# Attention followed by two feed-forward layers: clamp, value parts and value means of the attention rewritten

## The chip, the cores and the metric

One core of a Trainium2 chip runs the whole program. The time is device microseconds of one execution; three runs of the kernel before gave 818.24, 821.07 and 824.56 us, median 821.07. The engines are PE (TensorE matmul; PEld is its weight load), DVE (VectorE), ACT (ScalarE), POOL (GpSimd) and SP, which issues all DMAs. SBUF is the working memory, PSUM holds what matmuls write (here eight banks of 512 columns, the tile `bank`).

## The reference

Sixteen heads (2 batches of 8) of 768 tokens and 64 columns. Each query and key is assigned to the nearest of 16 centroids of its head, and a query only sees keys of its own cluster:

```
mask   = q_assign[:, :, :, None] == k_assign[:, :, None, :]
scores = scale * np.matmul(q, k.transpose(0, 1, 3, 2))
scores = np.where(mask, scores, -1000000000.0)
scores = scores - np.max(scores, axis=-1, keepdims=True)
attn   = np.exp(scores)
attn   = attn / (np.sum(attn, axis=-1, keepdims=True) + 1e-09)
x      = np.matmul(attn, v)
```

A query whose cluster holds no key sees all its scores equal, so its output is the mean of v. The result, 1536 tokens by 512, then goes through two layers `g(x @ w_in) @ w_out` with 2048 hidden columns, the first with a PReLU, the second with a rational function.

## The kernel before, in words

**Staging.** The program is a list of operations that a planner written into the kernel (`Sched`) puts in order when the program is built. Each operation names the engines that may run it, a cost on each, and the buffers that it takes. The planner places the operation whose planned start, weighted with a due time (`SC.t`), comes first, and among several engines it takes the one with the earliest planned end plus a bias. `BIAS` adds a fixed amount to DVE wherever DVE is one of several choices. What comes out is one fixed order per engine, and each engine works through its own in order. So a change of one cost, buffer or bias can move rows on every engine.

**Attention, one head `i` after the other.** `operands1`/`operands2` bring queries, keys, one-hot clusters into SBUF tiles by DMA. `max_chunk` (nine per head) multiplies 512 columns into a bank and reduces their maxima on DVE (L665) into the small tile `mp`. `m_chain` reduces `mp` to one maximum per query (L674, `mx`), clamps it (L677, `nm`), marks rows without keys on POOL (L679, `nh`), transposes `nm` on PE (L682) and sends the negated row by DMA into the operand. `st_chunk` (nine per head) computes scores on PE (L705, L706) and their exponential on ACT (L710) into `p32`. `p_split` writes each 128x768 block as a float16 part and a float16 remainder: the cast (L414 on ACT, L416 on POOL) and the subtraction (L722), which may go to DVE or POOL; in this kernel all 96 went to POOL. `pv_tile` (six per head, 18 matmuls each, L790 to L792) multiplies both parts with the value parts, and `pv_fin` divides: L807, L809 and L810 make the reciprocal denominator `rc` from the sum of the row, L812 scales the result from PSUM, L814 overwrites rows without keys with the mean.

**Values, one pair of heads.** `v_split` squares v on ACT (L733), sums v per column on DVE (L737), sums over partitions on PE (L740), makes a power-of-two scale `am` (L745, L748, L751 on DVE, L752 and L755 on POOL), casts the scaled v to float16 (L765 on ACT or L767 on POOL) and takes the remainder on DVE (L770). `x_T` transposes the finished pair into x.

**Feed-forward.** 96 steps: `emit_h` (L1033, 12 matmuls of 512 columns) and `emit_y` (L1102, 12 matmuls), with the weights prepared by `w_prep` on ACT, DVE and POOL (L996, L1002, L1004, L1006, L1009, L1016). The first weights are prepared while the last heads of the attention still run, and a few `emit_h` matmuls stand in PE's order ahead of the last transposes of `x_T` (L830).

## Time and profile before

| | |
|---|---|
| median of three runs | 821.07 us (818.24 to 824.56) |
| profiled execution | 825.44 us, its span 823.4 us |
| granted PE clock, mean | 0.965 of full speed |
| busy share of the span | PE 93%, DVE 74%, ACT 69%, POOL 72% |
| chain that ended last, by line | L1102 31%, L1033 30% |

The profile is of one execution of its own. PE's ends are modelled, so a busy PE is not a PE at its peak; how fast it works is read from the distance between the starts of its matmuls. The heads can be followed on DVE by the sixteen L674 (one per head, 35.9 to 253.7 us) and L807 (68.3 to 301.4 us).

### The profile page before, as it was taken

What the parts mean: (1) busy time and instruction counts of PE and PEld (TensorE: products, weight loads), DVE (VectorE), ACT (ScalarE), POOL (GpSimd) and SP (SyncE); (2) the same over time, 40 slices, a digit from 0 to 9 for tenths busy, and PEclk for the clock granted to TensorE, in tenths of its full rate; (3) what the DMA queues carried; (4) which work ended last, traced back from release to release, by engine and by line L of the source; (5) the groups of instructions that cost most, each with busy time, mean ns of one, the idle gap of its engine ahead of it and who ended that gap; (6) DMA issues with size and microseconds to landing.
All of it is one profiled execution on the core that took longest, in us unless ns stands there. A gap on an engine that the chain in (4) does not pass through costs nothing.

```text
span 823.4 us, 13646 instructions
## 1 busy us (share of the span) xinstructions
PE 768.9 (93%) x5103; PEld 636.6 (77%) x5103; DVE 606.6 (74%) x884; ACT 570.4 (69%) x1002; POOL 596.2 (72%) x496
## 2 busy tenths in 40 slices
PE   7888888999878579999999999999999999999997
PEld 6667767878757458888888888888888888888885
DVE  5695979899786867865455365358889889987775
ACT  3377869888877757765564465579989788767662
POOL 4077659778677999987575476689889789877443
PEclk9888989999989889999999999999999999999999
DMA  8653737667435222333131032021111111000012
GB/s 166 138 102 84 154 72 167 129 132 165 109 70 168 86 95 81 111 117 102 52 103 52 30 99 78 26 67 62 52 42 61 52 51 52 1 0 1 2 52 102
DMA packets 57858, 67.56 MB, mean 82 GB/s; under 512 B 27232, under 2 KB 46272, under 8 KB 57792
## 3 DMA queue, kind: packets, MB, share of 16 engines
q1 hardware_dynamic: 57792, 66.69, 31.2%
q8 instruction: 40, 0.66, 0.3%
q14 instruction: 26, 0.21, 0.1%
HBM read 43.04 MB, written 3.15 MB: 56 GB/s over the span
## 4 chain that ended last, share of the span: by engine, by line
PE 61%; DVE 1%; POOL 1%; issue 1%; ACT 0%; DVEq 0%; POOLq 0%
PE bank L1102 31%; PE bank L1033 30%; DVE arena_p L1044 0%; POOL arena_p L1061 0%; POOL arena_r L1079 0%; POOL arena_p L722 0%; DVE arena_p L1121 0%; DVE rc L810 0%; PE bank L792 0%; DVE arena_p L1006 0%; PE bank L790 0%; PE bank L791 0%; PE bank L830 0%; DVE bank L1044 0%; ACT arena_r L414 0%
## 5 line engine op out<-in xcount | busy, mean ns | idle before, releaser
L1102 PE MATMUL bank<-arena_r 128*128 128x512 f32 x1152 | 278.5, 390 | 8.8 <-ACT arena_r L414 8.4
L1033 PE MATMUL bank<-x,arena_r 128*128 128x512 f32 x1152 | 278.5, 391 | 0.4 <-POOL arena_r L1016 0.4
L1102 PEld LDWEIGHTS bank<-arena_r 128*128 128x128 f32 x1152 | 216.3, 188 | 55.4 <-ACT arena_r L414 9.2
L1033 PEld LDWEIGHTS bank<-x,arena_r 128*128 128x128 f32 x1152 | 216.7, 188 | 46.1 <-POOL arena_r L1016 1.1
L722 POOL TENSOR_TENSOR arena_p<-arena_p 128x768 f16<-128x768 f32 x96 | 162.8, 1716 | 31.1 <-ACT arena_p L414 27.3
L1079 POOL TENSOR_TENSOR arena_r<-arena_p,arena_r 128x512 fp32r<-128x512 f32 x96 | 133.4, 1390 | 52.2 <-ACT arena_r L414 41.9
L414 ACT CAST arena_r<-arena_p 128x512 fp32r<-128x512 f32 x133 | 80.8, 620 | 48.8 <-DVE arena_p L1044 29.4
L665 DVE TENSOR_REDUCE mp<-bank 128x1 f32<-128x512 f32 x144 | 92.0, 680 | 25.9 <-PE bank L659 25.6
L1044 DVE SCALAR_TENSOR_TENSOR arena_p<-arena_p,nal 128x512 f32<-128x512 f32 x48 | 54.2, 1130 | 70.2 <-ACT arena_p L1047 70.1
L1016 POOL TENSOR_TENSOR arena_r<-arena_p,arena_r 128x512 fp32r<-128x512 f32 x64 | 88.6, 1388 | 19.4 <-ACT arena_r L414 18.6
L1009 POOL TENSOR_TENSOR arena_p<-arena_p 128x512 int32<-128x512 int32 x64 | 90.6, 1418 | 11.1 <-ACT arena_p L1002 7.1
L710 ACT ACTIVATE arena_p<-bank 128x512 f32<-128x512 f32 x144 | 79.7, 594 | 23.0 <-PE bank L706 14.6
L1004 DVE TENSOR_SCALAR arena_p<-arena_p 128x512 uint32<-128x512 uint32 x64 | 61.4, 961 | 41.3 <-ACT arena_p L996 41.3
L705 PE MATMUL bank<-arena_r 128*128 128x512 f32 x192 | 70.1, 382 | 14.2 <-DVE mp L665 6.0
L1061 POOL TENSOR_TENSOR arena_p<-arena_p 128x512 f32<-128x512 f32 x48 | 62.7, 1309 | 26.7 <-ACT arena_p L1058 26.6
L1006 DVE SCALAR_TENSOR_TENSOR arena_p<-arena_p 128x512 uint32<-128x512 uint32 x64 | 75.2, 1174 | 1.1
L414 ACT CAST arena_p<-arena_p 128x768 f16<-128x768 f32 x93 | 74.5, 838 | 0.3
L706 PE MATMUL bank<-arena_r 128*128 128x512 f32 x192 | 65.0, 352 | 0.0
L790 PE MATMUL bank<-arena_p 128*128 128x65 f16 x576 | 63.4, 199 | 1.1 <-DVE arena_p L812 1.1
L1044 DVE SCALAR_TENSOR_TENSOR arena_p<-arena_p,cq,bank 128x512 f32<-128x512 f32 x48 | 35.8, 745 | 38.9 <-ACT bank L1069 31.8
L792 PE MATMUL bank<-arena_p 128*128 128x65 f16 x576 | 62.5, 198 | 1.3 <-POOL arena_p L722 1.1
L791 PE MATMUL bank<-arena_p 128*128 128x64 f16 x576 | 62.7, 197 | 0.0
(121 smaller groups left out, 1247.2 us busy)
## 6 DMA issues: line engine op xcount, KB each, us to landing
arena_p<-in_moe_w_in SPq DMA_DIRECT2D x32, 512.0 KB, 3.6
arena_p<-in_moe_w_out SPq DMA_DIRECT2D x32, 512.0 KB
arena_r<-arena_r SPq DMA_DIRECT2D x24, 384.0 KB, 4.0
arena_r<-arena_r SPq DMA_DIRECT2D x24, 192.0 KB, 5.4
arena_p<-in_q SPq DMA_DIRECT2D x8, 384.0 KB, 5.3
arena_p<-in_k SPq DMA_DIRECT2D x8, 384.0 KB, 7.0
...
```

The lines of the kernel that those rows point to most:

```text
L414: e.copy(o_, i_)
L665: op(dvep(CH), lambda e: e.reduce_max(mp.v[:, n0:n0 + np_], ps.v.rearrange("p (a k) -> p a k", a=np_), axis=AX.X), r=[ps], w=[(mp, c)])
L705: e.matmul(o_, lhsT=b_.v[:, 1, ks], rhs=b_.v[:, 0, lo:hi], start=True, stop=False)
L710: op(act_p(CH), lambda e: e.activation(p32.v.rearrange("p a s -> p (a s)")[:, cc * CH:(cc + 1) * CH], ps.v, ACTF.Exp, scale=scale), r=[ps] ...
L722: lambda e: e.tensor_sub(pt_.v[:, 1, :], src(), pt_.v[:, 0, :]),
L1006: op(dve2(N), lambda e, d0=d0, hi=hi: e.scalar_tensor_tensor(u(d0), hi(), 0x80000000, u(d0), op0=ALU.bitwise_and, op1=ALU.bitwise_or), r=[ ...
L1009: op(pool2(N), lambda e, d0=d0, d1=d1: e.tensor_tensor(n32(d0), n32(d0), n32(d1), op=ALU.add), r=[d0, d1], w=[d0])
L1016: lambda e, wt=wt, pick=pick, src=src: e.tensor_tensor(pick(wt.v)[:, 1], src(), f32(pick(wt.v)[:, 0]), op=ALU.subtract),
L1033: e.matmul(ps.v, lhsT=wi.v[:, wi_, kk, :], rhs=x[kk][:, xi, cols], start=n == 0, stop=n == 3 * KD - 1)
L1044: lambda e: e.scalar_tensor_tensor(o_.v, a_.v, sc, b_.v, op0=p0, op1=p1))
L1079: op([dve2(N), pool2(N)], lambda e: e.tensor_tensor(gg.v[:, 1, :], G.v, f32(gg.v[:, 0, :]), op=ALU.subtract), r=[G, (gg, 0)], w=[(gg, 1)])
L1102: e.matmul(ps.v, lhsT=lhsT, rhs=rhs, start=first and wi_ == gi == 0, stop=last and gi == 1)
```

## The change

1. The clamp: `mp` gets a third column per row block that always holds -2^59, so that the maximum already contains the clamp; `nm` and L677 go away, PE transposes `mx` itself, and the subtracted constant is added when the row is negated on ACT. POOL's mark tests `<=` in place of `<`.
2. Value parts: ACT writes scaled v into a PSUM bank (of the ring `S`, which max, score and other chunks use as well), then the float16 copy and the subtraction read that bank. The scale's two POOL steps become one, and it now lies between the DVE step that cuts the exponent and the DVE reciprocal.
3. Value means: the column sum L737 and the copy of the means go away. Twelve more matmuls per head multiply the value parts with a constant tile `level` of 256 and leave the sums in columns 390 to 454 of the bank that the head's result goes to.
4. `pv_fin`: rows without keys are overwritten in PSUM, sums and count together, before the division; the denominator takes two steps (the addition and the scale in one) in place of three.
5. The planner's numbers: the bias of DVE goes from 1.8311 to 1.0, and five costs of PE rise by some per cent.

```diff
-BIAS = {"DVE": 1.8311, "POOL": 0.0}
+BIAS = {"DVE": 1.0, "POOL": 0.0}
...
+    level = const.tile([P, P], F16, name="level")
+    nc.vector.memset(level, PSC)
...
-                           ("nh", 3, T, F32), ("nm", 2, T, F32), ("rc", 2, T, F32),
+                           ("nh", 3, T, F32), ("rc", 2, T, F32),
...
+    for s in SC.slots["mp"]:
+        nc.vector.memset(s.view.rearrange("p (t a) -> p t a", a=3)[:, :, 2], -BIG / 2)
...
         op((DVE, 0.09), lambda e: e.reduce_max(
-            mx.v, mp.v.rearrange("p (t a) -> p t a", a=2), axis=AX.X),
+            mx.v, mp.v.rearrange("p (t a) -> p t a", a=3), axis=AX.X),
            r=[(mp, c) for c in range(NCH)], w=[mx])
-        op((DVE, 0.07), lambda e: e.tensor_scalar(
-            nm.v, mx.v, -BIG / 2, LNP / scale, op0=ALU.max, op1=ALU.subtract), r=mk, w=[nm])
-        op((POOL, 0.3), lambda e: e.tensor_scalar(nh.v, mx.v, -BIG / 2, None, op0=ALU.is_lt),
-           r=mk, w=[nh])
+        op((POOL, 0.19), lambda e: e.tensor_scalar(nh.v, mx.v, -BIG / 2, None, op0=ALU.is_le),
+           r=[mx], w=[nh])
         nohas[i] = nh
-        op((PE, 0.11), lambda e: e.transpose(ps.v[:T, :P], nm.v, idf), r=[nm], w=[ps])
+        op((PE, 0.11), lambda e: e.transpose(ps.v[:T, :P], mx.v, idf), r=[mx], w=[ps])
...
-        op((DVE, 1.4), lambda e: e.reduce_sum(
-            vr.v[:, :2 * D].rearrange("p (h d) -> p h d", h=2),
-            raw.v.rearrange("p h t d -> p h d t"), axis=AX.X), r=[raw], w=[(vr, 2)])
-        op((PE, 0.3), lambda e: e.matmul(ps.v[:, :2 * D + 2], lhsT=ones, rhs=vr.v, start=True,
-                                         stop=True), r=[(vr, i) for i in range(3)], w=[ps])
-        op([(ACT, 0.17), (DVE, 0.2)], lambda e: (e.mul(vm_.v, ps.v[:, :2 * D], 1.0 / S)
...
-        op((DVE, 0.1), lambda e: e.tensor_scalar(
-            am.v[:, 2:4], ps.v[:, 2 * D:2 * D + 2], 2.0 ** -120, None, op0=ALU.max),
-           r=[ps], w=[am])
-        op((DVE, 0.1), lambda e: e.tensor_scalar(
-            am.v[:, 2:4].bitcast(U32), am.v[:, 2:4].bitcast(U32), 1, 0x7F800000,
-            op0=ALU.logical_shift_right, op1=ALU.bitwise_and), r=[am], w=[am])
+        op((PE, 0.22), lambda e: e.matmul(ps.v[:, :2], lhsT=ones, rhs=vr.v, start=True,
+                                          stop=True), r=[(vr, i) for i in range(2)], w=[ps])
+        op((DVE, 0.08), lambda e: e.tensor_scalar(
+            am.v[:, 2:4].bitcast(U32), ps.v[:, :2].bitcast(U32), 1, 0x7F800000,
+            op0=ALU.logical_shift_right, op1=ALU.bitwise_and), r=[ps], w=[am])
+        op((POOL, 0.19), lambda e: e.tensor_scalar(
+            am.v[:, 2:4], am.v[:, 2:4], 2.0 ** -124, 2.0 ** 50, op0=ALU.max, op1=ALU.mult),
+           r=[am], w=[am])
         op((DVE, 0.1), lambda e: e.reciprocal(am.v[:, 0:2], am.v[:, 2:4]), r=[am], w=[am])
...
-            op([act_s(384, 1), dve1(384), pool1(384, 1)], cvt, r=[raw, am], w=[(d, h, 1)])
-            op(dve2(384), lambda e, h=h, sc=sc, hi=hi, lo=lo: e.scalar_tensor_tensor(
-                lo(), raw.v[:, h], sc(), hi(), op0=ALU.mult, op1=ALU.subtract),
-               r=[raw, am, (d, h, 1)], w=[(d, h, 0)])
+            pv_ = SC.buf("S", "v")
+            pr = lambda pv_=pv_: pv_.v[:, :384].rearrange("p (t d) -> p t d", t=T)
+            op(act_s(384, 1), lambda e, h=h, sc=sc, pr=pr: e.activation(
+                pr(), raw.v[:, h], ACTF.Copy, scale=sc()), r=[raw, am], w=[pv_])
+            op([act_p(384), dvep(384)], lambda e, pr=pr, hi=hi: copy(e, hi(), pr()),
+               r=[pv_], w=[(d, h, 1)])
+            op(dvep(384), lambda e, pr=pr, hi=hi, lo=lo: e.tensor_tensor(
+                lo(), pr(), hi(), op=ALU.subtract), r=[pv_, (d, h, 1)], w=[(d, h, 0)])
...
+            def sums(e):
+                for kt in range(T):
+                    e.matmul(ps.v[:, 390:455], lhsT=level, rhs=d.v[:, e_, kt, 64:129],
+                             start=kt == 0, stop=False)
+                    e.matmul(ps.v[:, 390:454], lhsT=level, rhs=d.v[:, e_, kt, 0:64],
+                             start=False, stop=kt == T - 1)
+
+            op((PE, 0.36), sums, r=[(d, e_, 0), (d, e_, 1), (d, "one")], w=[(ps, T)])
...
-        op((DVE, 0.07), lambda e: e.tensor_scalar(rc.v, ps()[:, :, 64], PSC * 1e-9, None,
-                                                  op0=ALU.add), r=pk, w=[rc])
+        op(dvep(390), lambda e: e.copy_predicated(
+            ps(), nh.v.bitcast(U32).unsqueeze(2).to_broadcast([P, T, D + 1]),
+            ps_.v[:, 390:455].unsqueeze(1).to_broadcast([P, T, D + 1])),
+           r=[nh, (ps_, T)] + pk, w=pk)
+        op((DVE, 0.08), lambda e: e.tensor_scalar(
+            rc.v, ps()[:, :, 64], PSC * 1e-9, am.v[:, e_:e_ + 1], op0=ALU.add, op1=ALU.mult),
+           r=pk + [am], w=[rc])
         op((DVE, 0.11), lambda e: e.reciprocal(rc.v, rc.v), r=[rc], w=[rc])
-        op((DVE, 0.07), lambda e: e.tensor_scalar(rc.v, rc.v, am.v[:, 2 + e_:3 + e_], None,
-                                                  op0=ALU.mult), r=[rc, am], w=[rc])
...
-        op(dve2(384), lambda e: e.copy_predicated(
...
-        op((PE, 2.6), mm, r=[(wi, 0), (wi, 1)] + [
+        op((PE, 2.724), mm, r=[(wi, 0), (wi, 1)] + [
...
-            op((PE, 0.434), mm, r=[(wo, 0), (wo, 1), (gg, 0)], w=[ps])
+            op((PE, 0.454), mm, r=[(wo, 0), (wo, 1), (gg, 0)], w=[ps])
```

**How the order moves.** In the changed kernel the lines have other numbers: the subtraction of `p_split` is L725 (L722 before), the maximum `mx` L677 (L674), the overwriting of rows L803 (L814), the scaling of the result L811 (L812), the value remainder L758 (L770).

DVE where the third head is finished and the next maximum made. Before, small steps on `nm` and `rc` and the value remainder of the pair stand here:

```order
L807 TENSOR_SCALAR rc_119<-bank 128x6
L674 TENSOR_REDUCE mx_111<-mp_113 128x6
L838 TENSOR_TENSOR x<-bank,x 128x512
L838 TENSOR_TENSOR x<-bank,x 128x256
L770 SCALAR_TENSOR_TENSOR arena_p<-arena_p,am_123 128x6x64
L677 TENSOR_SCALAR nm_118<-mx_111 128x6
L809 RECIPROCAL rc_119<-rc_119 128x6
L810 TENSOR_SCALAR rc_119<-rc_119,am_122 128x6
L812 TENSOR_TENSOR arena_p<-bank,rc_119 128x6x64
```

and now:

```order
L803 COPY_PREDICATED bank<-nh_118,bank 128x390
L677 TENSOR_REDUCE mx_113<-mp_115 128x6
L807 TENSOR_SCALAR rc_119<-bank,am_122 128x6
L810 RECIPROCAL rc_119<-rc_119 128x6
L811 TENSOR_TENSOR arena_p<-bank,rc_119 128x6x64
L725 TENSOR_TENSOR arena_p<-arena_p 128x768
L532 TENSOR_TENSOR arena_r<-bank,arena_r 128x512
L669 TENSOR_REDUCE mp_114<-bank 128x1
L669 TENSOR_REDUCE mp_114<-bank 128x2
```

The steps with `nm` and `rc,am` are gone, the overwriting stands first and works in the bank, and one subtraction of `p_split`, 768 elements from SBUF and SBUF, has come onto DVE.

POOL from the mark of the last head on. Before:

```order
L679 TENSOR_SCALAR nh_114<-mx_109 128x6
L722 TENSOR_TENSOR arena_p<-arena_p 128x768 x4
L1009 TENSOR_TENSOR arena_p<-arena_p 128x512 x2
L722 TENSOR_TENSOR arena_p<-arena_p 128x768
L1016 TENSOR_TENSOR arena_r<-arena_p,arena_r 128x512 x2
L722 TENSOR_TENSOR arena_p<-arena_p 128x768 x2
L1009 TENSOR_TENSOR arena_p<-arena_p 128x512 x2
L1016 TENSOR_TENSOR arena_r<-arena_p,arena_r 128x512 x2
L722 TENSOR_TENSOR arena_p<-arena_p 128x768 x3
L1009 TENSOR_TENSOR arena_p<-arena_p 128x512
```

and now:

```order
L680 TENSOR_SCALAR nh_116<-mx_111 128x6
L725 TENSOR_TENSOR arena_p<-arena_p 128x768 x2
L1004 TENSOR_TENSOR arena_p<-arena_p 128x512
L416 TENSOR_SCALAR arena_r<-arena_p 128x512
L1011 TENSOR_TENSOR arena_r<-arena_p,arena_r 128x512
L1004 TENSOR_TENSOR arena_p<-arena_p 128x512
L416 TENSOR_SCALAR arena_r<-arena_p 128x512
L1011 TENSOR_TENSOR arena_r<-arena_p,arena_r 128x512
L1004 TENSOR_TENSOR arena_p<-arena_p 128x512
L725 TENSOR_TENSOR arena_p<-arena_p 128x768
L1011 TENSOR_TENSOR arena_r<-arena_p,arena_r 128x512
L1004 TENSOR_TENSOR arena_p<-arena_p 128x512
```

Of the subtractions that stand behind the last mark, 12 before, 4 are left on POOL, and the weight preparation (L1009 and L1016 before, L1004 and L1011 now) comes sooner. Over the whole program 63 of the 96 stay on POOL and 33 go to DVE: 3 ahead of the first head's end, 23 between there and the 13th, 7 behind. POOL takes 27 of the casts of 128x768 in place of 3, ACT 69 in place of 93.

DVE around the scale `am` of a pair. Before:

```order
L745 TENSOR_SCALAR am_123<-bank 128x2
L812 TENSOR_TENSOR arena_p<-bank,rc_120 128x6x64
L748 TENSOR_SCALAR am_123<-am_123 128x2
L665 TENSOR_REDUCE mp_113<-bank 128x1
L751 RECIPROCAL am_123<-am_123 128x2
L665 TENSOR_REDUCE mp_113<-bank 128x2
L665 TENSOR_REDUCE mp_113<-bank 128x1 x2
L665 TENSOR_REDUCE mp_113<-bank 128x2
```

and now:

```order
L741 TENSOR_SCALAR am_123<-bank 128x2
L669 TENSOR_REDUCE mp_115<-bank 128x1
L669 TENSOR_REDUCE mp_115<-bank 128x2
L669 TENSOR_REDUCE mp_115<-bank 128x1
L580 TENSOR_TENSOR arena_p<-arena_p,lmw_110 128x384
L747 RECIPROCAL am_123<-am_123 128x2
L669 TENSOR_REDUCE mp_115<-bank 128x1
L669 TENSOR_REDUCE mp_115<-bank 128x2
L669 TENSOR_REDUCE mp_115<-bank 128x1
L758 TENSOR_TENSOR arena_p<-bank,arena_p 128x6x64 x2
```

The reciprocal (L751 before, L747 now) came two rows behind a DVE step that it needs; now it needs POOL's new step (L744), which needs L741, and four rows of other DVE work stand between L741 and L747.

## Rows read from the trace of the kernel before

**Rows 1.** Windows, three stretches: start:end us, length, then busy us of PE, PEld, DVE, ACT, POOL.

```profile
68.40:253.70 185.30, 164.13 (x1970) 138.59 (x1970) 157.53 (x282) 147.00 (x278) 133.75 (x106) 0.94 0.56 124
253.70:307.20 53.50, 36.89 (x431) 28.65 (x430) 40.02 (x45) 38.52 (x68) 50.41 (x34) 0.87 0.37 114
307.20:823.40 516.20, 510.71 (x2250) 421.69 (x2248) 361.06 (x467) 349.88 (x591) 380.93 (x299) 1.00 0.18 58
```

**Rows 2.** Timeline of PE in the feed-forward part: start us, us, what.

```profile
319.66 2.88 PE L1033 MATMUL bank<-x,arena_r 128*128 128x512 f32 x12
322.38 2.88 PE L1102 MATMUL bank<-arena_r 128*128 128x512 f32 x12
```

**Rows 3.** Waits of PE, 306.5 us to the end: us, times, longest.

```profile
PE bank L1102 <- ACT arena_r L414: 0.5, 1, 0.5
```

**Rows 4.** Lines of DVE, 68.4:253.7: busy us, mean ns | idle before, releaser.

```profile
L665 DVE TENSOR_REDUCE mp<-bank 128x1 f32<-128x512 f32 (+1 forms) x109 | 69.9, 681 | 20.4 <-PE bank L659 20.1
L770 DVE SCALAR_TENSOR_TENSOR arena_p<-arena_p,am 128x384 f16<-128x384 f32 x14 | 17.4, 1252 | 0.0
L810 DVE TENSOR_SCALAR rc<-rc,am 128x6 f32<-128x6 f32 x12 | 10.2, 852 | 0.1
L814 DVE COPY_PREDICATED arena_p<-nh,arena_p 128x384 f32<-128x384 uint32 x12 | 9.8, 819 | 0.0
L737 DVE TENSOR_REDUCE arena_p<-arena_p 128x128 f32<-128x768 f32 x6 | 9.1, 1514 | 0.0
L677 DVE TENSOR_SCALAR nm<-mx 128x6 f32<-128x6 f32 x12 | 8.9, 741 | 0.0
...
L812 DVE TENSOR_TENSOR arena_p<-bank,rc 128x384 f32<-128x384 f32 x12 | 6.7, 558 | 0.2
```

**Rows 5.** Timeline of DVE, a passage at 100:124.

```profile
102.88 1.89 DVE L770 SCALAR_TENSOR_TENSOR arena_p<-arena_p,am 128x384 f16<-128x384 f32 x1
104.70 1.60 DVE L677 TENSOR_SCALAR nm<-mx 128x6 f32<-128x6 f32 x1
...
106.42 1.48 DVE L810 TENSOR_SCALAR rc<-rc,am 128x6 f32<-128x6 f32 x1
```

**Rows 6.** Timeline of POOL in the same passage.

```profile
99.16 8.70 POOL L722 TENSOR_TENSOR arena_p<-arena_p 128x768 f16<-128x768 f32 x5
```

**Rows 7.** Timeline of PE in the same passage; the bracket is idle time before.

```profile
106.35 0.27 PE L682 MATMUL bank<-idf,nm 128*6 128x128 f32 x1 [2.00 <-DVE nm L677]
```

**Rows 8.** Line L810, whole span: ns minimum/median/maximum.

```profile
L810 DVE TENSOR_SCALAR rc<-rc,am x16: 216/1036/1705, 68.9 to 302.7; 128x6 f32<-128x6 f32 x16
```

**Rows 9.** Line L1006, whole span: ns minimum/median/maximum.

```profile
L1006 DVE SCALAR_TENSOR_TENSOR arena_p<-arena_p x64: 678/1106/2027, 251.4 to 725.1; 128x512 uint32<-128x512 uint32 x64
```

**Rows 10.** Lines of POOL, 68.4:253.7.

```profile
L722 POOL TENSOR_TENSOR arena_p<-arena_p 128x768 f16<-128x768 f32 x73 | 122.5, 1699 | 27.7 <-ACT arena_p L414 24.2 <-PE bank L659 2.1 <-PE bank L706 0.5
...
L416 POOL TENSOR_SCALAR arena_p<-arena_p 128x768 f16<-128x768 f32 x2 | 1.7, 832 | 5.2 <-ACT arena_p L710 5.2
```

**Rows 11.** Lines of ACT over the whole span, shapes kept apart.

```profile
L414 ACT CAST arena_p<-arena_p 128x768 f16<-128x768 f32 x93 | 74.5, 838 | 0.3
...
L414 ACT COPY arena_p<-bank 64x384 f32<-64x384 f32 x16 | 7.4, 471 | 8.6 <-PE bank L550 8.4
```

**Rows 12.** Timeline of PE, first and last matmul of one value tile.

```profile
140.25 0.19 PE L790 MATMUL bank<-arena_p 128*128 128x65 f16 x1
...
140.77 0.20 PE L792 MATMUL bank<-arena_p 128*128 128x65 f16 x1
```

**Rows 13.** Lines of POOL, 253.7:307.2.

```profile
L722 POOL TENSOR_TENSOR arena_p<-arena_p 128x768 f16<-128x768 f32 x14 | 25.3, 1827 | 3.8 <-ACT arena_p L414 3.7
```

**Rows 14.** Lines of DVE, 253.7:307.2.

```profile
L814 DVE COPY_PREDICATED arena_p<-nh,arena_p 128x384 f32<-128x384 uint32 x4 | 5.2, 1304 | 0.0
L810 DVE TENSOR_SCALAR rc<-rc,am 128x6 f32<-128x6 f32 x4 | 4.9, 1222 | 0.1
```

**Rows 15.** Windows, the shortest period of a head.

```profile
151.30:163.50 12.20, 12.20 (x166) 10.79 (x166) 10.01 (x24) 11.42 (x21) 9.90 (x9) 1.00 0.31 70
```

More of the change, by code (lines that the diff above doesn't have):

```diff
@@ L751, in v_split @@
[L751 to L757 removed]
+                accum_out=vr.v[:, h:h + 1]), r=[raw], w=[(vr, h), junk])
+        op((PE, 0.22), lambda e: e.matmul(ps.v[:, :2], lhsT=ones, rhs=vr.v, start=True,
+                                          stop=True), r=[(vr, i) for i in range(2)], w=[ps])
@@ L802, in pv_fin @@
             xns[j] = SC.buf("xn")
-        xn, vm_, am = xns[j], vmean[j], vinv[j]
+        xn, am = xns[j], vinv[j]
         pk = [(ps_, t) for t in range(T)]
```

54 lines of the change are left out of this document (19 added, 35 removed).

## The prediction

> **What bounds the kernel now.** I read the stretches first [rows 1]. From 307.2 us on PE is busy 510.7 of 516.2 us: the feed-forward part is bound by PE alone. Its groups of 12 matmuls follow each other at a distance of 2.72 us [rows 2], so one matmul costs 0.227 us, and PE waits only 0.5 us more in that whole part [rows 3]. The change touches none of these matmuls, and 192 such groups take 522 us whatever comes before. So only the time until PE gets there can change: the heads, 68.4 to 253.7 us (12 periods of 15.4 us), and the tail, in which the last heads finish while POOL prepares weights.
>
> In the heads no engine is full: PE is busy 164 of 185 us, DVE 158, ACT 147, POOL 134 [rows 1]. What the reader is to see is how DVE spends its time. Beside 69.9 us of maxima it has 55 us in small steps that take far longer than their size: L810 handles 6 elements in 852 ns on the mean, L677 6 elements in 741 ns, L770 384 elements in 1252 ns, while L812, as many elements read from PSUM, takes 558 ns [rows 4]. A passage shows why: POOL runs five subtractions without a gap from 99.16 to 107.9 us [rows 6], and in that time DVE's L770, L677 and L810 take 1.89, 1.60 and 1.48 us [rows 5], each about one POOL operation long, while L810's shortest is 0.216 us [rows 8]. PE then stands 2.00 us for `nm` [rows 7]. So these steps wait for POOL, on SBUF. The Trainium skill, SBUF — State Buffer, section "Who interferes with whom", names the cause: a DVE step with two SBUF inputs, or a `tensor_scalar` in a two-port mode, shares a port pair with POOL, and the second to start is blocked until the first ends. The trace agrees, by L810's 0.216 to 1.705 us.
>
> In the tail POOL is busy 50.4 of 53.5 us, DVE 40.0, ACT 38.5, PE 36.9 [rows 1]: here POOL's row sets the pace, with 25.3 us in 14 subtractions of `p_split` [rows 13].
>
> **The change, part by part.** Times are for the 12 heads unless I say otherwise.
>
> *DVE, removed.* L677: 8.9 us. L810: 10.2. L737: 9.1. L770 becomes a subtraction from a bank, priced as L812, 14 x 0.558 = 7.8 in place of 17.4: 9.6 less. L814 moves into the bank, 390 elements, no row shows that form; between L812's 0.558 and twice that (two inputs from one bank) I take 0.558, since every 384-element row from PSUM lies there: 12 x 0.558 = 6.7 in place of 9.8, 3.1 less (at the upper end 3.6 more). Sum: 40.9 us less [rows 4].
>
> *DVE, added.* The lower bias sends 33 of the 96 subtractions to DVE, 23 of them in these heads. This form on DVE is not in the trace: 768 elements, both inputs in SBUF. Undisturbed: 384 elements take 0.558 and 512 take 0.681 us [rows 4], 512 with two SBUF inputs 0.678 at the least [rows 9]; 0.96 ns per element more gives 0.93 us. Its wait for POOL is nothing at best and a whole POOL operation, 1.70 us [rows 10], at worst, so 0.93 to 2.63 us each. The like steps waited on the mean 0.64 (L810, 0.852 less 0.216) and 0.69 us (L770 less 0.558). POOL itself gets emptier: 23 x 1.70 = 39 us less, about 20 casts of 0.83 us more [rows 10], so 111 us in place of 134; I scale 0.65 us to 0.54. Price 1.47 us, 23 of them 33.8 us (21.4 to 60.5).
>
> *Net on DVE:* 33.8 - 40.9 = -7.1 us (-19.5 to +19.6). All other engines but PE get lighter by more than that or about as much: POOL by 23 us; ACT gives away about 20 casts of 0.838 and gains 14 copies of 0.471 us [rows 11], 10 us less. So I take DVE's figure for the heads: **-7.1 us**.
>
> *PE.* Twelve more matmuls per head at (140.77 - 140.25)/17 = 0.031 us [rows 12] are 0.37 us, 4.4 us in the heads. I set this at nothing: PE has 21 us without work there [rows 1] and no longer stands for `nm`. Without that cover it costs 4.4 us.
>
> *The scale `am`.* DVE's reciprocal now needs a POOL step. If POOL is in a subtraction, that comes up to 1.70 us late, and DVE's next maxima and the value remainders queue behind the reciprocal. Its cover is the rows that stand between, in the piece shown three maxima and a 384-element step, 3 x 0.68 + 0.56 = 2.6 us, so I set it at nothing; without cover it costs 6 x 1.70 = 10 us. The two value banks per pair come out of the ring that scores and maxima share, held over three steps of about 0.5 us each; nothing, since that ring serves 18 chunks per head and one value bank per head is added. SP's order changes by a few neighbouring DMAs; nothing.
>
> *The tail.* Behind the last mark POOL keeps 4 subtractions in place of 12: 8 x 1.83 = 14.6 us less, POOL near 36. DVE gets 7: + 10.3 us at 1.47, and loses L810's 4.9 and 5.2 - 4 x 0.558 = 3.0 of L814 [rows 14]: 42.4 us in place of 40.0. So DVE becomes the fullest, and the tail cannot shrink below 42.4 of its 53.5 us, 11 us less. With the full wait, 2.63 each, DVE would need 50.5 and nothing is gained. I take two thirds of the room, **-7.5 us** (-11 to 0): the weight preparation goes ACT, DVE, POOL in turn and does not pack fully.
>
> *Feed-forward work done early.* Ahead of the last transposes PE's order has 54 matmuls of the feed-forward part before, 36 now. 18 x 0.227 = **+4.1 us** come behind them.
>
> Sum: -7.1 - 7.5 + 4.1 = -10.5 us. Against the profiled execution, 825.4 us, that is 814.9; this execution lies 4.4 us above the median of the runs, 821.1, so the forecast is **811 us**. Its own range, from the bounds that can go together, is 802 to 819.
>
> **The rivals.**
>
> *Off the path, 25%.* DVE waits 20.1 us for PE's max chunks in the heads [rows 4], so PE is at times the late one. Then DVE's relief becomes longer waiting, the heads gain nothing and pay the 4.4 us of sums; the tail still gains: +4.4 - 7.5 + 4.1 = +1.0, **822 us**. For it: PE's 164 of 185 us. Against it: DVE's blocked steps are what PE waited for in the passage.
>
> *VectorE swallows it, slower, 13%.* The change is meant to take pairs off SBUF, but its 33 subtractions are the largest SBUF pairs that DVE has had in a head, and they run beside POOL's own. The place is DVE's row, with the maxima behind each. From 40.9/23 = 1.78 us each on, the heads get longer. At 2.2 us: 50.6 - 40.9 = +9.7, the tail gains 3 at most, +4.1: **832 us**; at the full 2.63, with nothing gained in the tail, +24, 845 us. The rule of the Trainium skill quoted above speaks for this and against the change, since it gives the pair to whichever starts first for the whole instruction. By that rule taken at its worst the sum is that of the full price. Against the full price: blocked steps so far waited 0.65 us on the mean, not 1.70.
>
> *The chain opens, 10%.* The shortest head takes 12.20 us at full clock, with PE busy throughout [rows 15]. If all heads ran so, plus 0.37: 12 x 12.57 = 151 in place of 185 us, -34; the tail at its bound, -11; +4.1: **780 us**. Against it: DVE's maxima and the rest remain, and DVE hardly gets lighter.
>
> *The forecast* has 52%.
>
> **How the numbers follow.** About 1%, 8 us, is what a measurement here can tell; the three runs span 6.3 us. Faster by over 1% is below 812.9. The forecast's case lies below it with 36 of its 52%, the opened chain with its 10: 46%. Same: 16 from the forecast, 23 of the 25 off the path: 39%. Slower: 13 and 2: 15%. The range 798 to 828 leaves out the opened chain and about 10 of the 13% in which DVE swallows it.
>
> **What would show it.** In the profile of the changed kernel: the new subtraction on DVE (L725) at 1.3 to 1.7 us on the mean; above 1.8 the slower rival is right. DVE's busy time between the first and the 13th head some 7 us lower, and that stretch near 178 us; if DVE's waits for PE grow from 20 us instead, it is off the path. POOL below 85% in the tail and the last transposes (L825) near 292 us on PE in place of just before 307.2. The overwriting L803 near 0.56 us. The feed-forward part still at 2.72 us per group; if it now waits for weights, the gain of the tail is lost, which I have not priced, and the prediction is wrong there.

## The result

The changed kernel takes **798.76 us** (median of 4 runs, 795.59 to 800.81) against 822.72 us for the kernel before in the same session (4 runs, 818.24 to 824.56). The ratio is 0.971, with a 95% interval of 0.966 to 0.977: 24 us less, where 10.5 us had been forecast. The time lies at the lower end of the stated range of 798 to 828 us; the direction was right, and the gain that was forecast is less than half of the measured one.

Where it went is read from the stretches of [rows 1], here with the start as one more: up to the first `tensor_scalar` of a head's denominator (L807), from there to the 13th (the heads), to the last transposes (L825, the tail), to the end. This is the windows view of the changed kernel, profiled at 800.81 us; the columns are those of [rows 1], and the number behind POOL is the granted clock of PE as a share of full speed.

```profile
0.00:63.15 63.15, 56.35 (x479) 47.69 (x480) 44.85 (x98) 35.77 (x72) 28.20 (x54) 0.89 0.67 139
63.15:235.59 172.44, 161.82 (x2137) 140.03 (x2136) 141.86 (x265) 140.08 (x267) 121.04 (x99) 0.98 0.60 132
235.59:278.00 42.41, 31.88 (x415) 26.25 (x414) 36.02 (x41) 29.08 (x51) 36.52 (x27) 0.84 0.41 122
278.00:799.00 521.00, 515.09 (x2271) 425.24 (x2269) 380.93 (x474) 357.71 (x603) 385.38 (x296) 1.00 0.19 59
```

With the same marks the profile of before has 68.3, 185.2, 53.3 and 516.5 us. So the start is 5.2 us shorter, the heads 12.8, the tail 10.9, and the feed-forward part 4.5 longer: 24.4 us of span. The start's share can't be put down to the change, as a repeat shows. Each kernel was profiled once more (the runs are labelled as repeats below): this is the windows view of the kernel before, repeated, and then of the changed kernel, repeated.

```profile
0.00:61.55 61.55, 53.04 (x456) 43.53 (x457) 46.11 (x93) 34.21 (x69) 30.97 (x60) 0.97 0.68 141
61.55:247.14 185.59, 164.59 (x1970) 139.24 (x1969) 157.85 (x280) 146.93 (x277) 134.00 (x106) 0.94 0.57 124
247.14:300.50 53.36, 37.37 (x432) 29.18 (x430) 40.12 (x46) 38.59 (x68) 50.25 (x34) 0.84 0.37 114
300.50:817.00 516.50, 510.99 (x2253) 422.10 (x2250) 361.00 (x467) 351.06 (x591) 381.68 (x299) 1.00 0.18 58
```

```profile
0.00:61.41 61.41, 52.64 (x479) 44.75 (x480) 44.79 (x98) 35.28 (x71) 28.45 (x54) 0.94 0.69 143
61.41:233.99 172.58, 162.12 (x2139) 140.07 (x2136) 141.89 (x266) 139.99 (x267) 121.00 (x99) 0.98 0.60 132
233.99:274.70 40.71, 29.04 (x415) 24.12 (x414) 36.92 (x41) 28.96 (x51) 36.58 (x27) 0.92 0.41 123
274.70:795.60 520.90, 515.07 (x2271) 425.27 (x2269) 380.90 (x474) 356.92 (x603) 384.97 (x296) 1.00 0.19 59
```

Here both starts take 61.5 us, the heads differ by 13.0 us and the tail by 12.7. The start varies from run to run, and the clock granted in it with it (the kernel before: 68.3 us at 0.88, 61.55 us at 0.97); heads and feed-forward part repeat within 0.4 us, the changed kernel's tail within 1.7. So below I compare heads and tails, and take the whole from medians.

In the heads, DVE's lines answer [rows 4]; this is the view of its lines in the changed kernel, 63.15 to 235.59 us.

```profile
L669 DVE TENSOR_REDUCE mp<-bank 128x1 f32<-128x512 f32 (+1 forms) x108 | 69.4, 685 | 17.7 <-PE bank L663 17.7
L725 DVE TENSOR_TENSOR arena_p<-arena_p 128x768 f16<-128x768 f32 x23 | 27.2, 1188 | 4.3 <-ACT arena_p L414 3.1 <-POOL arena_p L416 1.1
...
L803 DVE COPY_PREDICATED bank<-nh,bank 128x390 f32<-128x390 uint32 x12 | 6.7, 562 | 0.0
L811 DVE TENSOR_TENSOR arena_p<-bank,rc 128x384 f32<-128x384 f32 x12 | 6.7, 556 | 0.3
...
L758 DVE TENSOR_TENSOR arena_p<-bank,arena_p 128x384 f16<-128x384 f32 x12 | 6.1, 552 | 0.4 <-ACT arena_p L414 0.4
```

The 23 moved subtractions (L725) cost 1.19 us each, not 1.47. The overwriting in the bank (L803) takes 0.562 us, as priced, and the value remainder (L758) 0.552. The same operations one by one: the view of single lines gives minimum, median and maximum over the whole span.

```profile
L725 POOL TENSOR_TENSOR arena_p<-arena_p x63: 1633/1655/2339, 45.3 to 264.2; 128x768 f16<-128x768 f32 x63
...
L725 DVE TENSOR_TENSOR arena_p<-arena_p x33: 915/960/2415, 43.2 to 264.8; 128x768 f16<-128x768 f32 x33
...
L680 POOL TENSOR_SCALAR nh<-mx x16: 225/524/1007, 33.8 to 237.8; 128x6 f32<-128x6 f32 x16
```

The medians hide two groups, which the single instructions of this trace show. 18 of DVE's 33 subtractions began with no POOL operation under way, or with one that had less than 0.2 us to run, and took 0.915 to 0.976 us. The other 15 met one that had 0.28 to 1.60 us to run; they ended 0.80 to 0.82 us behind it and took 1.10 to 2.42 us. In the heads these were 7 of 23. POOL now pays too: eight of its 16 comparisons of 6 elements, L680, began while a DVE subtraction ran and took 0.81 to 1.01 us, the other eight took 0.225 to 0.238, so that the median of 0.524 us is the time of none of them; the counterpart before (L679) had a median of 0.226. One place shows both, in the timeline of DVE and then of POOL:

```profile
124.60 1.66 DVE L725 TENSOR_TENSOR arena_p<-arena_p 128x768 f16<-128x768 f32 x1
...
123.78 1.66 POOL L725 TENSOR_TENSOR arena_p<-arena_p 128x768 f16<-128x768 f32 x1
125.53 0.82 POOL L680 TENSOR_SCALAR nh<-mx 128x6 f32<-128x6 f32 x1
```

DVE's subtraction begins while POOL's runs and ends 0.8 us behind it; the comparison that POOL begins meanwhile ends when DVE is done.

PE's waits in the heads, which answer [rows 7], are two rows now (waits view: us, times, longest); the third row is the one of [rows 7] in the same view of the kernel before:

```profile
PE bank L663 <- DMA arena_r<-arena_r: 7.5, 5, 2.5
PE bank L663 <- ACT arena_p L414: 3.0, 1, 3.0
...
PE bank L682 <- DVE nm L677: 4.0, 3, 2.0
```

PE no longer waits for the clamped maxima. Before, DVE ended 15.8 of PE's 21.1 us of waiting in the heads, in nine rows of this view; now it ends none of 10.5. And the feed-forward part still goes at 2.72 us per group, as in [rows 2]; the timeline of PE in the changed kernel:

```profile
283.59 2.88 PE L1028 MATMUL bank<-x,arena_r 128*128 128x512 f32 x12
286.31 2.88 PE L1097 MATMUL bank<-arena_r 128*128 128x512 f32 x12
```

### The profile page after: what moved, and what is told of

Read it like the earlier page. It is cut to its first block, busy times and chain, and to the rows that moved or that the text cites. A ratio compares the mean times of both kernels' runs of the same rounds, so it can differ in the third digit from the quotient of the medians.

```text
span 799.0 us, 13995 instructions
## 1 busy us (share of the span) xinstructions
PE 765.1 (96%) x5295; PEld 639.2 (80%) x5295; DVE 603.7 (76%) x874; ACT 562.6 (70%) x990; POOL 571.1 (71%) x473
## 4 chain that ended last, share of the span: by engine, by line
PE 86%; DMA 4%; DVE 3%; ACT 2%; issue 2%; SPq 1%; POOL 1%; DVEq 0%; ACTq 0%; POOLq 0%
PE bank L1028 32%; PE bank L1097 32%; PE bank L663 4%; PE bank L708 4%; PE bank L709 3%; DMA arena_r<-arena_r 3%; PE bank L786 2%; PE bank L788 2%; PE bank L787 2%; PE bank L552 2%; ACT arena_p L713 1%; DMA arena_p<-in_q 1%; DVE arena_p L725 1%; ACT arena_p L414 1%; PE bank L525 1%
## 5 line engine op out<-in xcount | busy, mean ns | idle before, releaser
L1074 POOL TENSOR_TENSOR arena_r<-arena_p,arena_r 128x512 fp32r<-128x512 f32 x96 | 131.9, 1374 | 38.8 <-ACT arena_r L414 17.2
L725 POOL TENSOR_TENSOR arena_p<-arena_p 128x768 f16<-128x768 f32 x63 | 108.4, 1728 | 25.4 <-ACT arena_p L414 23.5
L1004 POOL TENSOR_TENSOR arena_p<-arena_p 128x512 int32<-128x512 int32 x64 | 91.1, 1428 | 29.1 <-ACT arena_p L997 16.0
L1011 POOL TENSOR_TENSOR arena_r<-arena_p,arena_r 128x512 fp32r<-128x512 f32 x64 | 93.5, 1463 | 14.5 <-ACT arena_r L414 13.7
L1039 DVE SCALAR_TENSOR_TENSOR arena_p<-arena_p,nal 128x512 f32<-128x512 f32 x48 | 53.2, 1110 | 53.8 <-ACT arena_p L1042 53.4
L1001 DVE SCALAR_TENSOR_TENSOR arena_p<-arena_p 128x512 uint32<-128x512 uint32 x64 | 86.3, 1348 | 1.6
L663 PE MATMUL bank<-arena_r 96*128 96x512 f32 x192 | 52.9, 373 | 11.6 <-DMA arena_r<-arena_r 8.4
```

Of the source, the lines that this page charges most:

```text
L725: lambda e: e.tensor_sub(pt_.v[:, 1, :], src(), pt_.v[:, 0, :]),
L1004: op(pool2(N), lambda e, d0=d0, d1=d1: e.tensor_tensor(n32(d0), n32(d0), n32(d1), op=ALU.add), r=[d0, d1], w=[d0])
L1011: lambda e, wt=wt, pick=pick, src=src: e.tensor_tensor(pick(wt.v)[:, 1], src(), f32(pick(wt.v)[:, 0]), op=ALU.subtract),
L1039: lambda e: e.scalar_tensor_tensor(o_.v, a_.v, sc, b_.v, op0=p0, op1=p1))
L1074: op([dve2(N), pool2(N)], lambda e: e.tensor_tensor(gg.v[:, 1, :], G.v, f32(gg.v[:, 0, :]), op=ALU.subtract), r=[G, (gg, 0)], w=[(gg, 1)])
```

## The experiments

**Theory P**: the steps that wait for POOL stand on PE's chain; taking them out gives the gain, and the moved subtractions help only the tail. **Theory B**: the subtractions moved to DVE give the gain. The ratios stand against the kernel before in the same session, with the 95% interval. "Order kept" means that the planner was given the costs of the kernel that was edited, so every other instruction stays where it was.

### The small steps taken out of the kernel before, order kept

First the clamp alone: a constant third column in `mp`, and the transposes read `mx`.

```diff
-        op((DVE, 0.07), lambda e: e.tensor_scalar(
-            nm.v, mx.v, -BIG / 2, LNP / scale, op0=ALU.max, op1=ALU.subtract), r=mk, w=[nm])
...
```

> The kernel before with its order of rows kept, in which only the clamp is taken out of VectorE's row (the maximum contains it, the transpose reads the maximum itself). Theory P (steps that wait for GpSimd lie on the chain to TensorE and set the pace of the heads): the 12.0 us of L677 go, and most of them show, 5 to 10 us faster than before. Theory B (the 33 subtractions moved to VectorE give the gain, the small steps were cover): 0 to 2 us faster. Theory O (the newly planned order gives the gain): 0 to 2 us faster.

Measured: 814.65 us, 0.989 (0.984 to 0.995). Then the denominator's second step as well:

```diff
-        op((DVE, 0.07), lambda e: e.tensor_scalar(rc.v, rc.v, am.v[:, 2 + e_:3 + e_], None,
-                                                  op0=ALU.mult), r=[rc, am], w=[rc])
```

> As the one before, and the denominator in two steps too (L810 out, its factor in L807), order of rows kept. P: another 15.1 us of busy time go, 10 to 18 us faster than before in all. B: 0 to 3 us faster. O: 0 to 3 us faster.

Measured: 810.36 us, 0.985 (0.979 to 0.991). Then also the value means through the bank:

```diff
-        op((DVE, 1.4), lambda e: e.reduce_sum(
-            vr.v[:, :2 * D].rearrange("p (h d) -> p h d", h=2),
...
-        op(dve2(384), lambda e: e.copy_predicated(
-            xn.v[:, :, e_, :], nh.v.bitcast(U32).unsqueeze(2).to_broadcast([P, T, D]),
...
+                    e.matmul(ps.v[:, 390:455], lhsT=level, rhs=d.v[:, e_, kt, 64:129],
...
+            ps_.v[:, 390:455].unsqueeze(1).to_broadcast([P, T, D + 1])), e.tensor_scalar(
```

> As the one before, and the value means through PSUM too (column sum L737 out, twelve matmuls per head in, overwriting in the bank), order of rows kept; the value parts and the planner's numbers stay as before. P: 14 to 22 us faster than before. B: 0 to 4 us faster. O: 0 to 4 us faster, or slower by the 6 us of matmuls.

Measured: 805.21 us, 0.978 (0.974 to 0.982). No subtraction has moved, and three quarters of the gain are there. Last, the denominator's step alone, the clamp left in:

```diff
+            rc.v, ps()[:, :, 64], PSC * 1e-9, am.v[:, e_:e_ + 1], op0=ALU.add, op1=ALU.mult),
...
-        op((DVE, 0.07), lambda e: e.tensor_scalar(rc.v, rc.v, am.v[:, 2 + e_:3 + e_], None,
```

> The kernel before, order kept, with only the two-step denominator: L810's 6-element multiplication in SBUF is folded into the step that reads the bank, the clamp stays. Theory C (L810's waits stand on TensorE's chain, as the difference of the medians with and without it, 814.65 and 810.36, says): 816 to 820 us. Rival D (they lie beside it, as the stretches of these two kernels say, heads 176.3 and 176.0 us, tails 52.5): 821 to 825 us.

Measured: 811.56 us, 0.986 (0.984 to 0.989). Theory C expected 816 to 820: it falls short of the gain, and D is wrong. The heads of these four, windows view: clamp out, denominator's step out, both out, all three out.

```profile
63.05:239.35 176.30, 159.14 (x1970) 135.00 (x1969) 153.43 (x268) 146.65 (x277) 134.37 (x106) 0.98 0.57 130
```

```profile
68.39:243.00 174.61, 157.79 (x1972) 133.20 (x1971) 150.06 (x269) 147.14 (x278) 135.64 (x106) 0.99 0.60 133
```

```profile
69.27:245.30 176.03, 159.09 (x1970) 135.69 (x1969) 142.37 (x256) 146.07 (x277) 135.03 (x106) 0.97 0.59 131
```

```profile
63.81:235.13 171.32, 159.03 (x2116) 136.01 (x2115) 132.27 (x249) 145.63 (x271) 135.15 (x106) 1.00 0.60 134
```

Against 185.2 us before, either step alone gives 9 to 11 us, and both together give 9. They don't add up. (The medians of the runs, with their intervals, don't separate the three either.) DVE's busy time falls by 4.0, 7.4 and 15.1 us in the first three, and the heads don't follow it. What changes alike is PE: its busy time goes from 164.1 to 158 or 159 us for the same matmuls, with the granted clock from 0.94 to 0.97 and more, and its idle time from 21 to 17 us. With the value means out as well, the heads are 13.9 us shorter than before.

### Is it the waiting, or one more step?

The clamp replaced by a step of the same size in the same place of the chain, one that reads one column and has not waited in any run (the constant third column stays, as in the run with the clamp out):

```diff
-            nm.v, mx.v, -BIG / 2, LNP / scale, op0=ALU.max, op1=ALU.subtract), r=mk, w=[nm])
+        op((DVE, 0.07), lambda e: e.reduce_max(nm.v, mx.v.unsqueeze(2), axis=AX.X), r=mk, w=[nm])
```

> The kernel before, its order kept, with the clamp of 6 elements (L677) replaced by an equally small step in the same place of the chain that has not waited for GpSimd in any run: a maximum over one column, 6 elements in, 6 out, from which TensorE transposes. Theory W (the 0.741 us mean of L677 is waiting for GpSimd, and that waiting stands on TensorE's chain): the step takes 0.15 to 0.17 us and the time is that of the kernel without the clamp, 812 to 818 us. Rival S (any further step between the maxima and the transpose costs that much, by its own length and its semaphore): 819 to 824 us.

Measured: 813.23 us, 0.987 (0.985 to 0.989). The view of single lines of that kernel:

```profile
L679 DVE TENSOR_REDUCE nm<-mx x16: 145/150/161, 35.6 to 242.9; 128x6 f32<-128x6 f32 x16
```

The step is there, 0.145 to 0.161 us, where the clamp took 0.160 to 1.620, and the gain is that of taking it out: the heads take 176.6 us, against 176.3. So for the clamp it is the waiting. For whom, the trace of the kernel before tells: seven of its 16 clamps took 0.160 to 0.173 us, and the other nine, each begun while a POOL subtraction ran, all ended 0.03 us behind the end of that subtraction. L810 and L770 do the same: ten of 16 end 0.03 us, and ten of 16 some 0.42 us, behind a POOL operation. The Trainium skill, "SBUF — State Buffer", section "Who interferes with whom", says that a `tensor_reduce` never contends with GpSimd on trn2; the row of L679 agrees.

### The moved subtractions taken back, or made alone

The changed kernel with DVE's old bias, planned anew: all 96 subtractions on POOL.

```diff
-BIAS = {"DVE": 1.0, "POOL": 0.0}
+BIAS = {"DVE": 1.8311, "POOL": 0.0}
```

> The changed kernel with the bias of VectorE back at 1.8311: no subtraction of p_split on VectorE, all 96 on GpSimd, the order planned anew. P: 12 to 20 us of the 24 us of gain stay, 803 to 811 us. B: at most 8 us stay, 815 us or more. O: the order differs in some hundred rows, so anything between; it would say nothing for O alone.

Measured: 798.98 us, 0.972 (0.966 to 0.978): the time of the changed kernel, and better than P's 803 to 811. Its heads and tail, windows view:

```profile
62.84:226.49 163.65, 157.39 (x2100) 135.50 (x2099) 123.33 (x246) 148.05 (x283) 136.50 (x106) 1.00 0.64 143
226.49:276.30 49.81, 38.31 (x466) 31.62 (x466) 29.09 (x36) 37.28 (x66) 48.82 (x34) 0.86 0.32 97
```

Without them the heads are 8.8 us shorter than in the changed kernel, the tail 7.4 longer. PE is idle for 6.3 us in these heads and its clock is full; with the subtractions moved it is idle for 10.6, at 0.98. Theory B is out. Each of the two orders was planned anew, so more than the subtractions differs. In the kernel before, the bias alone:

```diff
-BIAS = {"DVE": 1.8311, "POOL": 0.0}
+BIAS = {"DVE": 1.0, "POOL": 0.0}
```

> The kernel before with only VectorE's bias lowered to 1.0, planned anew: 20 subtractions on VectorE, 14 of them in the heads and 6 in the tail, all the small steps that wait for GpSimd left in. Theory P (moved subtractions cost the heads, and help the tail only where the small steps are gone): 822 to 832 us. Theory B (the moved subtractions relieve GpSimd and with it the steps that wait for it): 808 to 817 us.

Measured: 820.20 us, 0.997 (0.995 to 0.999). Neither fits: a gain of 2.4 us, heads 178.5, tail 54.0. In this one profile the heads are 6.8 us shorter than before, although 13 subtractions have come onto DVE there: with the waiting steps still in, moving them did not cost the heads. Why the median gains less than the heads of the profile was not looked into. And value parts through PSUM alone, planned anew:

```diff
-            op(dve2(384), lambda e, h=h, sc=sc, hi=hi, lo=lo: e.scalar_tensor_tensor(
-                lo(), raw.v[:, h], sc(), hi(), op0=ALU.mult, op1=ALU.subtract),
...
+            op(dvep(384), lambda e, pr=pr, hi=hi, lo=lo: e.tensor_tensor(
+                lo(), pr(), hi(), op=ALU.subtract), r=[pv_, (d, h, 1)], w=[(d, h, 0)])
```

> The kernel before with only the value parts made through a bank of PSUM, planned anew. Theory P: L770's 17.4 us in the heads become about 7.8, and some of these waits stand on TensorE's chain: 3 to 7 us less, 815 to 819. Rival R (what separates the order-kept kernel at 805 from the one without moved subtractions at 799 is the planner's new order, not the value parts): 820 to 825.

Measured: 814.92 us, 0.989 (0.986 to 0.991), heads 173.3, tail 53.4. As with the other steps, the first one taken out gives some 9 us; here the order was planned anew, so it is not the wait alone.

More on DVE, the bias at 0.5:

```diff
-BIAS = {"DVE": 1.0, "POOL": 0.0}
+BIAS = {"DVE": 0.5, "POOL": 0.0}
```

> The changed kernel with VectorE's bias at 0.5: about 49 subtractions on VectorE in place of 33. Theory P (each one in the heads costs them time, in the tail they help): 800 to 808 us, heads 174 to 180. The slower rival of the prediction (VectorE swallows it): its subtractions wait longer, mean above 1.5 us, 808 us or more. Theory B (moved subtractions make the gain): 792 to 797 us.

Measured: 819.90 us, 0.996 (0.994 to 0.998). 77 subtractions went to DVE, not the 49 of the expectation, and P's 800 to 808 us is missed. The windows view of start and heads, and the line in the heads:

```profile
0.00:75.16 75.16, 66.27 (x622) 55.74 (x622) 57.26 (x114) 42.27 (x85) 25.20 (x54) 0.91 0.64 134
75.16:255.19 180.03, 161.40 (x1969) 134.45 (x1968) 161.53 (x290) 114.75 (x222) 70.84 (x77) 0.95 0.54 119
```

```profile
L725 DVE TENSOR_TENSOR arena_p<-arena_p 128x768 f16<-128x768 f32 x53 | 53.6, 1038 | 3.2 <-POOL arena_p L416 2.8 <-ACT arena_p L414 0.3
```

The 13th head is reached at 255.2 us, 19.6 later than in the changed kernel (12.0 of it in the start, 7.6 in the heads), and 21 us of the 24 are lost. The slower rival's time is met, but not by its longer waits: 53 subtractions at 1.04 us are 26.4 us more than the 23, with POOL at 71 of 180 us. The order moved as well: 622 matmuls stand ahead of the first mark, where the changed kernel has 479. How much is the number of subtractions and how much the order is not separated.

### The small steps put back into the changed kernel, its order kept

A clamp ahead of the transposes and a multiplication by 1.0 behind each reciprocal:

```diff
+            e.tensor_scalar(nmx[i % 3], mx.v, -BIG / 2, None, op0=ALU.max)),
...
+            e.tensor_scalar(rc.v, rc.v, 1.0, None, op0=ALU.mult)), r=[rc], w=[rc])
```

> The changed kernel in its own order, with two small SBUF steps put back on VectorE: a clamp of 6 elements ahead of each head's transpose, and a multiplication of 6 elements by 1.0 behind each reciprocal of the denominator. Theory P: they wait for GpSimd again and stand on TensorE's chain: 6 to 14 us slower, 805 to 813. Rival Q (in the new order GpSimd is emptier and these steps have cover, the gain comes from what was moved): 798 to 802.

Measured: 811.60 us, 0.987 (0.984 to 0.990): 12.8 us of the 24 are gone, heads 181.9, tail 43.0. P holds: the clamp takes 0.170 to 1.628 us there, the multiplication 0.170 to 1.657. An overwriting of 384 elements in SBUF instead:

```diff
+                                                 op=ALU.mult), e.copy_predicated(
+            xn.v[:, :, e_, :], nh.v.bitcast(U32).unsqueeze(2).to_broadcast([P, T, D]),
+            xn.v[:, :, e_, :])),
```

> The changed kernel in its own order with an overwriting of 384 elements in SBUF added behind each head's multiplication by the denominator (it writes the same values again, so it only costs its time, as L814 did before). Theory O (in the tail such an overwriting, late ahead of the last transposes, is what kept the tail at 53.5 us although subtractions were moved there): tail 47 to 52 us, 806 to 814 us. Rival Q (it is one more DVE step like others): about 1 us per head where PE waits for it, heads 1 to 6 us longer, tail below 45, 800 to 806 us.

Measured: 806.47 us, 0.980 (0.978 to 0.982), heads 174.9, tail 43.9. O is wrong for the tail; Q fits in heads and tail and misses its time by half a microsecond.

### The tail

The kernel before with only the last three heads' subtractions cheaper on DVE:

```diff
-        op([but(dve2(S), -0.1715), but(pool2(S), -0.0503)],
+        op([but(dve2(S), -0.1715 - (0.8311 if i >= 13 else 0.0)), but(pool2(S), -0.0503)],
```

> The kernel before with the subtractions of the last three heads alone made cheaper on VectorE, about 8 of them there; all blocked steps stay. Theory P: heads unchanged at 185 us, tail 6 to 9 us shorter than 53.3, and 2 to 4 us of that given back because fewer feed-forward matmuls are done ahead of the last transposes: 816 to 820 us. Theory B (the moved subtractions make the gain): 810 or less. If the blocked steps L677 and L810 set the tail too: no change, 822.

Measured: 821.98 us, 0.998 (0.995 to 1.001), tail 53.5 although POOL falls to 43.9 us in it. P missed that. Is it the waiting steps, or that planner's order? The same order without the three small steps (the edit above, in the kernel with all three out):

```diff
+        op([but(dve2(S), -0.1715 - (0.8311 if i >= 13 else 0.0)), but(pool2(S), -0.0503)],
```

> The order of the kernel before in which only the last three heads' subtractions are cheaper on VectorE (821.98 us, tail 53.5), kept, with the three small waiting steps taken out (clamp, denominator's second step, value means and their overwriting in SBUF). Theory O (the small steps kept that tail long): tail 44 to 47 us, against 50.3 with the small steps out and nothing moved, 797 to 801 us. Rival N (the order of work in that tail keeps it long, whatever the steps wait): tail 49 to 53 us, 803 to 808.

And the changed kernel with all three put back:

```diff
+            e.tensor_scalar(nmx[i % 3], mx.v, -BIG / 2, None, op0=ALU.max)),
...
+            e.tensor_scalar(rc.v, rc.v, 1.0, None, op0=ALU.mult)), r=[rc], w=[rc])
...
+                                                 op=ALU.mult), e.copy_predicated(
```

> The changed kernel in its own order with all three kinds of small waiting steps put back on VectorE (clamp, a multiplication behind the reciprocal, an overwriting of 384 elements in SBUF), the value parts and the moved subtractions staying. Theory O: together they bring the tail back to 49 us or more, 816 to 825 us in all. Rival N: tail 43 to 46, heads 182 to 186, 810 to 816 us.

Measured: 807.56 us (0.981, 0.977 to 0.984) and 813.15 us (0.987, 0.984 to 0.990). Their tails, windows view:

```profile
234.63:287.60 52.97, 36.48 (x471) 31.74 (x471) 41.68 (x46) 34.54 (x61) 42.16 (x33) 0.84 0.35 108
```

```profile
244.47:289.40 44.93, 29.61 (x394) 24.26 (x394) 39.13 (x48) 29.14 (x52) 37.06 (x26) 0.90 0.35 107
```

Without the steps that tail stays long, with all of them the changed kernel's stays short: N. So it goes with the order in which the planner then puts the work. What in that order does it was not tried, but PE's waits in the tails tell where to look. First the largest one of the kernel before, then the one of the long tail of 52.97 us, then two of the changed kernel:

```profile
PE bank L1102 <- ACT arena_r L414: 7.8, 1, 7.8
...
PE bank L798 <- DVE arena_p L726: 9.7, 4, 5.7
...
PE bank L788 <- POOL arena_p L725: 5.4, 1, 5.4
...
PE bank L788 <- DVE arena_p L725: 0.9, 2, 0.5
```

Before, six matmuls of `emit_y` stand in PE's order ahead of the last transposes, and PE waits 7.8 us for the cast that they need; POOL ends less than 2 us of PE's waits in that tail. In the changed kernel no `emit_y` matmul stands there. In the long tail the value matmuls wait for the moved subtractions (L726), which stand in DVE's row among the weight preparation. Neither reading was tested by a run.

### Subtractions moved in the last heads alone

The changed kernel with the old bias, and only the last three heads' subtractions cheaper on DVE:

```diff
-BIAS = {"DVE": 1.0, "POOL": 0.0}
+BIAS = {"DVE": 1.8311, "POOL": 0.0}
...
+        op([but(dve2(S), -0.1715 - (0.8311 if i >= 13 else 0.0)), but(pool2(S), -0.0503)],
```

> The changed kernel with VectorE's bias back at 1.8311 for everything but the subtractions of the last three heads, which keep the cheaper VectorE: none of them on VectorE in the heads, 7 in the tail. Theory P (the removed steps stood on TensorE's chain; subtractions moved to VectorE cost the heads and help only the tail): heads as without moved subtractions, 163.7 us, tail as in the changed kernel, 42 to 44, feed-forward part 520 to 521, so 789 to 794 us, faster than both 799s. Rival R (the 163.7 us were the luck of one order, and do not go together with a short tail): 797 to 803 us.

Then the last four:

```diff
+        op([but(dve2(S), -0.1715 - (0.8311 if i >= 12 else 0.0)), but(pool2(S), -0.0503)],
```

> As the kernel with VectorE's cheaper subtractions in the last three heads alone (793.7 us), but in the last four: 11 of them. Theory P (they cost where heads follow each other and help where only the tail is left): 793 to 797 us, the further ones falling into the last period of the heads. Rival (the further ones help as much as the first): 789 to 792 us.

Measured: **793.70 us**, 0.965 (0.962 to 0.968), and **793.81 us**, 0.965 (0.962 to 0.967). The first one's heads and tail:

```profile
64.00:230.32 166.32, 158.71 (x2114) 136.43 (x2114) 124.81 (x247) 149.43 (x286) 138.02 (x107) 1.00 0.64 142
230.32:274.00 43.68, 34.67 (x450) 28.94 (x449) 37.23 (x40) 33.64 (x60) 41.08 (x28) 0.88 0.32 95
```

It has the short heads and the short tail. By medians that is 5 us less than the changed kernel; the two were not timed in one session, and the intervals of their ratios overlap, so that it is faster than the changed kernel is likely but not shown.

### The repeats

No edit in either: the kernel before and the changed kernel once more.

> The kernel before once more, for the time of its first score chunk's denominator, 68.3 us in the profile shown. Theory S (the 5 us that the changed kernel is ahead by there are its own): 67 to 69 us. Rival V (the start depends on the clock that a run is granted in it, 0.88 against 0.92): anything from 63 to 69.

> The changed kernel once more, for the same mark, 63.1 us in its profile. Theory S: 62 to 64 us. Rival V: anything from 63 to 69.

Measured: 61.55 and 61.41 us to the first mark. S is out; V holds in that the start varies, though both lie below its 63; one run each, 819.02 and 797.34 us.

## Why the prediction was right about the direction and wrong about the size

**The mechanism of the small steps: right.** L677, L810 and L770 waited for POOL, as the ends of these steps in the trace show, and in the clamp's place a step that did not wait gave the whole gain of taking it out. For the other two steps that was not tried.

**The step that failed** is the one in the heads, as the prediction put it: "So I take DVE's figure for the heads: -7.1 us". It took the net change of DVE's busy time for the change of the heads. The figure itself was mis-sized: the added term came to 27.2 us in place of 33.8, since a subtraction took 1.19 us and not the price of 1.47. The price carried over the mean wait of the small steps; only 7 of the 23 met a POOL operation under way, and why so few was not looked into. With that, DVE's busy time fell by 157.5 - 141.9 = 15.6 us, and the heads by 12.8 to 13.0. But that these two numbers come close is luck, by the other runs. DVE's busy time does not set the length of the heads: with the clamp out it fell by 4.0 and the heads by 8.9; with both small steps out by 15.1 and 9.2; with the bias lowered alone it rose by 3.5 and the heads fell by 6.8; with all small steps out and nothing moved it fell by 34.1 and the heads by 21.6. The heads are made of PE's busy and idle time, 164.1 + 21.1 us before, 161.8 + 10.6 after, 157.4 + 6.3 with nothing moved. So the changed kernel's -12.8 can be read as the sum of two terms of opposite sign: -21.6 from the steps taken out (value parts and the new order with them), +8.8 from the subtractions moved in, with what the planner moved beside them. Two more runs agree in sign: with subtractions moved in the last three heads alone the heads took 166.3 us, with 53 moved in the heads 180.0, though in another order.

**The clock was not priced.** PE stands 2.00 us for `nm` [rows 7]. What came behind that wait is this passage of the kernel before, windows view:

```profile
100.00:104.00 4.00, 2.96 (x17) 1.92 (x14) 4.00 (x7) 3.88 (x8) 4.00 (x3) 1.00 0.94 220
104.00:108.00 4.00, 1.69 (x11) 0.94 (x9) 3.93 (x5) 0.93 (x4) 3.87 (x3) 0.90 0.34 100
108.00:112.00 4.00, 2.26 (x31) 1.96 (x32) 3.68 (x6) 3.73 (x8) 1.14 (x2) 0.50 0.00 1
112.00:116.00 4.00, 4.00 (x58) 3.48 (x55) 2.85 (x5) 1.11 (x3) 2.34 (x2) 0.75 0.01 4
```

PE is busy 1.69 of 4 us, with the wait of 2.00 us in it, and then the granted clock is at its lower level of 1.2 GHz for the next 4 us and part of those that follow. The kernel before has four such passages in its heads (from 72, 104, 208 and 240 us; its repeat has four too), the one without the clamp two, the one without the denominator's step one, the one without both two, the changed kernel two (its repeat one), and the ones with all small steps out or with nothing moved none. That fits the 9 to 11 us which the first waiting step taken out gives, whichever it is, while L810's waits above its shortest were 12 x 0.64 = 7.6 us in all: 5 to 6 us of the gain are busy time of PE, spent at the lower clock before (the value matmuls follow each other at 0.055 us from 110.3 us on, and at 0.031 us in [rows 12]). That the clock does this is read from the traces; no run held it fixed. How the waits group to make PE stand that long, and so which step is worth what beside another, was not isolated. The Trainium skill, "TensorE: Matmul & The Clock Gate", section "HAM oscillation — how this bites in real kernels", describes this cost, a wait paid once more as slow matmuls behind it; the passage agrees, with a clock of 0.50 behind the wait.

**The tail: right in place, short in size.** This term missed by as much as the one of the heads: -7.5 us was forecast (two thirds of a room of 11), -10.9 and -12.7 were measured, and by the repeats the heads missed by 5.9 us and the tail by 5.2. POOL came to 36.5 us, as forecast (36). The room had been taken from DVE at 42.4 us; it is 36.0 in fact. And the forecast's reason, that POOL's row sets the pace there, is not borne out: with POOL relieved in the kernel before nothing was gained, and of PE's waits in that tail POOL ended less than 2 us. What sets the length of the tail stays open.

**Feed-forward matmuls done early: right**, +4.1 forecast, +4.5 and +4.4 measured; the groups stay at 2.72 us. **The reciprocal behind POOL's new step: right**; the reciprocal takes 0.153 to 0.166 us, and the one wait for POOL's new step is 0.6 us of ACT. **The sums on PE** were set at nothing and were not taken out alone. **The start** was set at nothing, and the one pair of repeats has it so.

**The rivals.** "Off the path" is out: DVE's waits for PE went from 20.1 to 17.7 us, not up. "VectorE swallows it" did not happen at 33 subtractions; at 77 nearly the whole gain was gone, but the kernel was not slower than before, and the subtractions waited less than that rival needs (1.04 us on the mean, its bound is 1.78). "The chain opens" had the right eye for what more there was: with nothing moved, PE's idle time in the heads is down to 6.3 us. In sum, by the repeats: -13.0 - 12.7 + 4.4 - 0.1 = -21.4 us of span.
